# A rational MLP behind attention: the order of TensorE's products fixed by hand, in runs of one width

## The chip, the cores and the metric

One core of a Trainium2 chip runs the whole program. The metric is the device time of one execution in microseconds; the median of several runs counts. The engines are TensorE (matrix products, PE in the rows; its weight loads, PEld, overlap them), VectorE (DVE), ScalarE (ACT), GpSimd (POOL) and SyncE (SP), the last two issuing most of the DMAs.

## What is computed

Attention over 4 batches of 12 heads, 448 tokens and 64 columns a head, with a soft cap on the scores; its output, 1792 tokens by 768, goes through an MLP of 2048 hidden columns with a rational activation:

```python
x = attn_out.transpose(0, 2, 1, 3).reshape(B * S, H * D)   # 1792 x 768
h = x @ w_in                                               # 768 x 2048
P = a[0] + a[1] * h + a[2] * h * h + a[3] * h * h * h
Q = 1.0 + abs(b[0]) * abs(h) + abs(b[1]) * h * h
out = (P / (Q + 1e-6)) @ w_out                             # 2048 x 768
```

The change lies in the MLP. The two weight matrices come as 64-bit floats.

## The kernel before

All products keep nearly full precision by splitting each operand into a high and a low part and adding three products, high by high, high by low and low by high. The instructions of attention and MLP are first written down as operations with the keys that they read and write. `Plan.flush` (L118) then puts them in an order: it goes through a modelled time, and on each engine takes from the operations that are ready the one of smallest priority number, which is its place in the code less an `early`. Only the order comes from this; on the chip the engines wait for each other by semaphores.

**First stage.** The hidden columns are cut into 16 blocks of 128, two to a group g, and the tokens into two halves m of 896. A *unit* is one block of one half: `units` (L270) runs over g, then m, then the block y in the group, 32 units, four to a group. `stage1` (L764) computes a unit transposed, 128 hidden columns by 896 tokens: 6 pieces kc of the contraction, three products each, and each product for the token columns 0 to 512 and 512 to 896, because one product writes at most one of PSUM's banks. So a unit is 36 matmuls (L782), a 512-column and a 384-column one alternating, into two banks of one of the tiles `PS[0]`, `PS[1]`, `PS[2]` (`hbuf`, L787). Each kc is one operation of six matmuls, so that the plan can put other work between.

**Activation.** `rational` (L791) reads a unit from PSUM and makes G, high and low, in SBUF: six ScalarE and seven VectorE operations over 128x896 (L813 to L826), among them a logarithm (L818) and an exponential (L820) for the division.

**Second stage.** `stage2` (L828) computes one output *tile* of 128 tokens by 768 columns from the two units of a pair (the two blocks of one group and half): per block six matmuls of 384 columns (L851). There are seven tiles to a half. Tiles take turns in PSUM: `PS[1]`, or the pair of single banks `pv` and `mi`. A tile of the first half is copied to an `ev` buffer by ScalarE (L878), and a DMA on GpSimd's queue adds it to the output in memory; there are three such buffers. A tile of the second half is added to an accumulator in SBUF by VectorE (L884), or in the first group copied by ScalarE (L881).

**Weights.** `load_w` (L688) brings a weight tile as 64-bit words to one raw buffer by an SP DMA; `make_w` (L708) turns it into a 32-bit float (ScalarE L729, VectorE L731, L734, L737), and `split_w` (L752) writes its high half (ScalarE L759) and low half (VectorE L761) to a place in a ring of three for w_in or w_out.

**The order.** `mlp` (L902) writes units 0 and 1, then for each unit: its first stage, its rational, some waiting tiles of an earlier pair, and the conversion and next load that the table `todo` (L929) gives for this unit. What TensorE then does is up to the plan.

Of the kernel before, what the change touches and what calls it, by code (L numbers as in the profile page):

```python
# [58 lines left out]
TAIL_NS = 870  # L59
D_NS = 1430  # L60
E_S2 = 30

# [176 lines left out]
class Body:  # L239
# [468 lines left out]
    def make_w(self, f, which, park=None):  # L708
# [7 lines left out]
        X, xk = self.X, ("x", "M")  # L716
        n = self.DM
        if self.wide:


            XI = X.bitcast(I32)
            rk = self.rslot[(f, which)]
            if rk[1] == "A":
                X, xk = self.XA, ("x", "A")
                XI = X.bitcast(I32)
            wds = self.raw[rk[1:]].rearrange("p (n t) -> p n t", t=2)
            lo, hi = wds[:, :, 0], wds[:, :, 1]
            self.op(ACT, act_ns(n, False),
                    lambda: nc.scalar.activation(X, hi.bitcast(F32), AF.Abs, scale=2.0 ** -111), [rk], [xk])  # L729
            self.op(DVE, dve_ns(n, fast=True),  # L730
                    lambda: nc.vector.tensor_scalar(XI, XI, 3, 0x7FFFFFFF, ALU.logical_shift_left, ALU.bitwise_and),  # L731
                    [], [xk])
            self.op(DVE, dve_ns(n),
                    lambda: nc.vector.scalar_tensor_tensor(XI, hi, -0x80000000, XI, ALU.bitwise_and, ALU.bitwise_or),  # L734
                    [rk], [xk])
            self.op(DVE, dve_ns(n),
                    lambda: nc.vector.scalar_tensor_tensor(XI, lo, 29, XI, ALU.logical_shift_right, ALU.bitwise_or),  # L737
                    [rk], [xk])
            if park is not None:
                self.dma(SP, self.w32[park], X, [xk], [("w32", park)])  # L740
                return
# [10 lines left out]
    def split_w(self, f, which, X, xk):  # L752
        nc = self.nc
        hl, hk = self.wtile(f, which)
        n = self.DM

        c = self.ws if which == "w_in" else 1.0
        whole = self.rings.pop(hk, [])
        self.op(ACT, act_ns(n, False), lambda: nc.scalar.mul(hl()[:, 0], X, c), [xk], [(*hk, 0)] + whole)  # L759
        self.op(DVE, dve_ns(n),  # L760
                lambda: nc.vector.scalar_tensor_tensor(hl()[:, 1], X, c, f32(hl()[:, 0]), ALU.mult, ALU.subtract),  # L761
                [xk, (*hk, 0)], [(*hk, 1)])

    def stage1(self, u):  # L764

# [7 lines left out]
        po = self.PS[i].rearrange("p a b -> p (a b)")  # L773
        parts = slice(0, 512), slice(512, 2 * self.S)
        for kc in range(KC):
            h, lo = ([t[m][kc][:, ts] for ts in parts] for t in (self.XH, self.XL))
# [14 lines left out]
    def rational(self, u):  # L791
        nc = self.nc
        c = self.c
# [6 lines left out]
        h = self.PS[s].rearrange("p a b -> p (a b)")[:, 0:n].rearrange("p (a b) -> p a b", a=2)  # L800
        hk = [("ps", s)]

# [25 lines left out]
    def stage2(self, g, m, t):  # L828
# [6 lines left out]
        tt = slice(128 * t, 128 * t + 128)  # L835
        last = g == self.NG - 1

        end = s == 1 and (m, g, t) == (self.B // 2 - 1, self.NG - 1, len(self.acc) - 1)
        halves = []
        for y in range(self.NCH):  # L840
# [15 lines left out]
            if not end:  # L856
                self.op(PE, 6 * 174, lambda run=run: run((0, 1)), keys, pk)
            else:
                halves.append((run, keys))
        for n in range(2 if end else 0):  # L860
            for run, keys in halves:
                self.op(PE, 3 * 174, lambda run=run, n=n: run((n,)), keys, pk[n:n + 1])
        acc, ws = self.acc[t], self.ws
        ie = self.nev % len(self.ev)
        ev = self.ev[ie]
# [36 lines left out]
    def mlp(self, rest):  # L902
# [22 lines left out]
        for kc in range(self.KC - 2, self.KC):  # L925
            self.split_x(1, kc)
        pend = []
        last = len(self.units) - 1
        todo = [[(("w_in", 2), ("w_out", 1), ("w_out", 2), ("w_in", 3))[2 * m + y]] for _, m, y in self.units]  # L929
        todo = [[(which, g * self.NCH + d) for which, d in l] for l, (g, _, _) in zip(todo, self.units)]  # L930
        todo[0], todo[1] = [("w_out", 0)], todo[1] + todo[0]
        for u, (g, m, y) in enumerate(self.units):
            if u > 1 and u < last:
                self.stage1(u)
            self.rational(u)
            if u == last - 1:
                self.stage1(last)
            k = len(pend) // (self.NCH - y)
            for a in pend[:k]:
                self.stage2(*a)  # L940
            pend = pend[k:]

            for which, f in todo[u]:
                self.make_w(f, which)
            for which, f in todo[u + 1][:1] if u < last else ():
                self.load_w(f, which)
            if y == self.NCH - 1:
                pend = [(g, m, t) for t in range(NTT)]
        for a in pend:
            self.stage2(*a)  # L950

    def memory(self):
# [83 lines left out]
        if self.wide:  # L1036
            t, o = take(2 * self.DM)
            keys("M", o, (("raw", "M", 0), 2 * self.DM))
            keys("P", o, (("parked", 0), self.DM), (("parked", 1), self.DM))
            self.raw["M", 0] = t.bitcast(I32)  # L1040

        t, o = take(896)
# [11 lines left out]
        self.X, o = take(self.DM)  # L1054
        keys("M", o, (("x", "M"), self.DM))


# [172 lines left out]
```

## Time and profile before

| | us |
|---|---|
| median of 3 runs | 674.99 |
| lowest, highest | 674.13, 675.17 |
| the profiled execution | 673.43 |
| its span, first to last instruction | 671.6 |
| TensorE busy | 658.4 (98%) |
| VectorE busy | 546.7 (81%) |
| ScalarE busy | 445.7 (66%) |

Attention runs to about 192 us, the MLP from there to the end. In each row of a timeline the first number is the start in us from the span's start and the second the length from there to the end of the last of the merged instructions; a bracket gives the engine's idle time ahead and what ended it. Matmuls overlap, so the busy time of TensorE says only that it has work; how fast it goes is read from the distance between starts. The line numbers in the rows are those of the code above.

### The profile page before, as it was taken

To read this page: it belongs to the slowest core of one execution; us is meant where nothing else is said; L and a number is where in the kernel's file an instruction comes from. 1 tells how busy PE (TensorE), PEld (TensorE's weight loads), DVE (VectorE), ACT (ScalarE), POOL (GpSimd) and SP (SyncE) were. 2 spreads that over 40 slices of the span, in tenths; PEclk is the share of its full clock that TensorE was granted. 3 is DMA by queue.
4 is the path that set the end of the run, shared out by engine and by line. 5 is a ranking of instruction groups with operands and counts; after the bars stand their busy time and mean duration, and the time that the engine had idled before them with its cause. 6 is when DMAs were issued, how large, how long until landed. Compare 5 with 4: busy or idle time off the path is not lost.

```text
span 671.6 us, 9841 instructions
## 1 busy us (share of the span) xinstructions
PE 658.4 (98%) x3852; PEld 542.5 (81%) x3852; DVE 546.7 (81%) x677; ACT 445.7 (66%) x531; POOL 97.0 (14%) x159
## 2 busy tenths in 40 slices
PE   7999999999999999999999999999999999999996
PEld 4555455555468899999999999999999999999996
DVE  4789899998869987887877997887799789779753
ACT  5799989998948867674476556447655644764560
POOL 4023323233200000120011012001101200110030
PEclk9999999999999999999999999999999999999999
DMA  7757767763131351482167129216712831670086
GB/s 175 173 127 163 171 158 157 145 138 95 30 104 29 124 182 48 88 151 68 56 154 144 48 57 184 66 51 159 143 47 58 157 92 51 160 143 0 1 128 207
DMA packets 79896, 74.44 MB, mean 111 GB/s; under 512 B 49377, under 2 KB 68065, under 8 KB 79841
## 3 DMA queue, kind: packets, MB, share of 16 engines
q1 hardware_dynamic: 68240, 48.68, 25.8%
q0 software_dynamic: 10448, 24.80, 21.8%
q8 instruction: 32, 0.52, 0.3%
q10 hardware_dynamic: 1152, 0.25, 0.2%
q14 instruction: 24, 0.19, 0.1%
HBM read 47.98 MB, written 25.65 MB: 110 GB/s over the span
## 4 chain that ended last, share of the span: by engine, by line
issue 57%; PE 24%; POOL 6%; ACT 5%; DMA 3%; DVE 3%; SPq 0%; ACTq 0%; POOLq 0%; DVEq 0%
PE ps L413 8%; POOL out_dram L286 6%; PE mi L497 4%; PE pv L497 3%; ACT etiles L443 2%; PE mi L542 2%; ACT ps L425 2%; PE ps L334 1%; PE pv L514 1%; DMA out_dram<-arena_f 1%; PE ps L851 1%; PE ps L357 1%; PE ps L782 1%; ACT arena_r L586 1%; DMA arena_f<-in_k_dram 1%
## 5 line engine op out<-in xcount | busy, mean ns | idle before, releaser
L782 PE MATMUL ps<-arena_r,ring 128*128 128x512 f32 (+1 forms) x1152 | 246.3, 368 | 0.0
L782 PEld LDWEIGHTS ps<-arena_r,ring 128*128 128x128 f32 x1152 | 209.4, 188 | 26.2 <-issue 0.7
L286 POOL DMA_DIRECT2D out_dram<-arena_f x49 | 43.1, 893 | 425.8 <-ACT arena_f L878 421.7
L851 PE MATMUL ps<-arena_r,etiles 128*128 128x384 f32 x462 | 90.0, 335 | 0.9 <-ACT arena_f L878 0.5
L825 ACT CAST etiles<-arena_f 128x896 fp32r<-128x896 f32 x32 | 30.1, 942 | 91.0 <-DVE arena_f L824 91.0
L425 ACT ACTIVATE ps<-ps 128x896 f32<-128x896 f32 x84 | 74.3, 907 | 19.4 <-PE ps L413 18.9
L851 PEld LDWEIGHTS ps<-arena_r,etiles 128*128 128x128 f32 x462 | 81.0, 188 | 2.6 <-ACT arena_f L878 0.9
L443 ACT ACTIVATE etiles<-ps,acap 128x896 f32<-128x896 f32 x84 | 82.4, 1011 | 1.1
L851 PE MATMUL pv<-arena_r,etiles 128*128 128x384 f32 x231 | 77.0, 335 | 0.0
L851 PE MATMUL mi<-arena_r,etiles 128*128 128x384 f32 x231 | 76.9, 334 | 0.0
L413 PE MATMUL ps<-arena_r 64*128 64x448 f32 x576 | 71.0, 380 | 4.5 <-DVE arena_r L342 2.0
L413 PEld LDWEIGHTS ps<-arena_r 64*128 64x128 f32 x576 | 50.6, 184 | 29.6 <-ACT etiles L443 6.8
L813 ACT ACTIVATE arena_f<-ps,b 128x896 f32<-128x896 f32 x32 | 32.3, 1009 | 40.7 <-PE ps L782 40.3
L817 DVE SCALAR_TENSOR_TENSOR arena_f<-arena_f,bab 128x896 f32<-128x896 f32 x32 | 36.7, 1147 | 24.4 <-ACT arena_f L814 24.3
L826 DVE TENSOR_TENSOR etiles<-arena_f,etiles 128x896 fp32r<-128x896 f32 x32 | 34.8, 1088 | 18.4 <-ACT etiles L825 17.6
L822 DVE SCALAR_TENSOR_TENSOR arena_f<-arena_f,one 128x896 f32<-128x896 f32 x32 | 36.7, 1148 | 16.0 <-ACT arena_f L820 15.9
L851 PEld LDWEIGHTS pv<-arena_r,etiles 128*128 128x128 f32 x231 | 43.3, 188 | 0.7
L851 PEld LDWEIGHTS mi<-arena_r,etiles 128*128 128x128 f32 x231 | 43.3, 188 | 0.0
L851 PE MATMUL ps<-ring,etiles 128*128 128x384 f32 x210 | 42.3, 336 | 0.2
L818 ACT ACTIVATE arena_f<-arena_f,qb 128x896 f32<-128x896 f32 x32 | 33.7, 1054 | 8.0 <-DVE arena_f L817 7.9
L851 PEld LDWEIGHTS ps<-ring,etiles 128*128 128x128 f32 x210 | 36.9, 188 | 1.3 <-ACT arena_f L878 0.8
L815 ACT ACTIVATE arena_f<-ps,a 128x896 f32<-128x896 f32 x32 | 35.4, 1106 | 3.5 <-DVE arena_f L823 3.5
(123 smaller groups left out, 1027.1 us busy)
## 6 DMA issues: line engine op xcount, KB each, us to landing
out_dram<-arena_f POOLq DMA_DIRECT2D x49, 384.0 KB, 6.0
arena_f<-in_moe_w_out_dram SPq DMA_DIRECT2D x16, 768.0 KB, 4.1
arena_f<-in_moe_w_in_dram SPq DMA_DIRECT2D x16, 768.0 KB, 6.0
out_dram<-arena_f SPq DMA_DIRECT2D x13, 384.0 KB, 3.2
ring<-in_q_dram SPq DMA_DIRECT2D x44, 112.0 KB, 4.3
arena_r<-dn POOLq DMA_DIRECT2D x20, 224.0 KB, 4.7
ring<-in_k_dram SPq DMA_DIRECT2D x33, 128.0 KB, 4.5
ring<-in_v_dram SPq DMA_DIRECT2D x11, 384.0 KB, 3.8
```

Source lines behind the costliest of these rows:

```text
L286: self.op(eng, (625 if local else 450) if eng == SP else 1050, lambda: e.dma_start(out, in_, **accum), r, w, nbytes=nbytes, **kw)
L413: m = nc.tensor.matmul(self.PS[i][:, j, 0:448], st[r], mv[r], start=y == 0, stop=y == len(ops) - 1)
L425: self.op(ACT, act_ns(896, True), lambda: nc.scalar.activation(ps, ps, AF.Tanh), ["table"], pk)
L443: self.op(ACT, act_ns(size, sk[0][0] == "ps", 1), lambda: nc.scalar.activation(e, src, AF.Exp, scale=acap), sk + ["table"], [ek])
L497: m = nc.tensor.matmul(po[64 * j:64 * j + 64, 0:448], raw["v"][:, 2 * x + j, 64 * c:64 * c + 64], tiles[c][0][:, j], start=c == 0, stop=False)
L782: r = nc.tensor.matmul(po[:, ts], w[:, y, kc], x, start=kc == 0 and z == 0, stop=kc == KC - 1 and z == 2)
L815: self.op(ACT, act_ns(n, True, 2), lambda: T.activation(A, h, AF.Identity, scale=a[:, 3:4], bias=a[:, 2:3]), hk, ak)
L817: self.op(DVE, dve_ns(n, 1), lambda: stt(Bt, C, bab[:, 1:2], Bt, ALU.mult, ALU.add), ck + ["bab"], bk)
L818: self.op(ACT, act_ns(n, False, 1), lambda: T.activation(C, Bt, AF.Ln, scale=TWO_M64, bias=qb), bk + tb, ck)
L822: self.op(DVE, dve_ns(n, 1), lambda: stt(Bt, Bt, one, C, ALU.add, ALU.mult), ck, bk)
L826: self.op(DVE, dve_ns(n), lambda: V.tensor_tensor(GL(), A, f32(GH()), ALU.subtract), ak + K("gh", ig), K("gl", ig))
L851: r = nc.tensor.matmul(po[n][:, 0:384], st, mv[:, 384 * n:384 * n + 384], start=(y == 0 and x == 0), stop=(y == self.NCH - 1 and x == 2))
```

## The change

Units from 4 on issue all 18 products of 512 columns first and then the 18 of 384, each as one operation. Behind each run a fixed number of second-stage tiles follows (`PER`: two and two, but none and three behind every fourth unit, one left over before it). These operations and the tiles share a key `turn`, so the plan may not change their order on TensorE. A pair's tiles are queued when the second unit behind it begins. Of a group's w_out tiles, one is converted in the group's first unit and one in its third, ahead of that unit's rational, which is about a unit later than before; conversions get an `early` of 10. The last group's tiles of the first half have six `ev` buffers in place of three, in memory of the raw buffer and of `X`.

```diff
+E_W = 10
+PER = ((2, 2), (2, 2), (2, 2), (0, 3))
+LAST = (0, 0)
+FIRST = 3
...
+        early = E_W * (park is None and f >= len(EARLY))
...
-    def stage1(self, u):
+    def stage1(self, u, between=None):
...
+        if between:
+            for x, ts in enumerate(parts):
+                def run(ts=ts):
+                    w = wi().rearrange("p s (k f) -> p s k f", f=128)
+                    for kc in range(KC):
+                        h, lo = (t[m][kc][:, ts] for t in (self.XH, self.XL))
+                        for z, (y, mv) in enumerate(((0, h), (0, lo), (1, h))):
+                            r = nc.tensor.matmul(po[:, ts], w[:, y, kc], mv,
+                                                 start=kc == 0 and z == 0, stop=kc == KC - 1 and z == 2)
+                    return r
+                self.op(PE, 18 * (174, 229)[x == 0], run,
+                        [(*wk, 0), (*wk, 1)] + [(n, m, kc) for n in ("xh", "xl") for kc in range(KC)],
+                        [(("ps", "psb")[x], i), "turn"])
+                between(x)
+            return
...
-        hk = [("ps", s)]
+        hk = [("ps", s), ("psb", s)]
...
+        turn = [] if not g and not m else ["turn"]
...
-        ie = self.nev % len(self.ev)
+        ie = (t + 3) % 6 if last else self.nev % 3
...
-        todo = [[(("w_in", 2), ("w_out", 1), ("w_out", 2), ("w_in", 3))[2 * m + y]] for _, m, y in self.units]
-        todo = [[(which, g * self.NCH + d) for which, d in l] for l, (g, _, _) in zip(todo, self.units)]
-        todo[0], todo[1] = [("w_out", 0)], todo[1] + todo[0]
+        todo = [(("w_out", 0), ("w_in", 2), ("w_out", 1), ("w_in", 3))[2 * m + y] for _, m, y in self.units]
+        todo = [(which, g * self.NCH + d) for (which, d), (g, _, _) in zip(todo, self.units)]
+        tiles = []
+
+        def pop(n):
+            for a in tiles[:n]:
+                self.stage2(*a)
+            del tiles[:n]
+
         for u, (g, m, y) in enumerate(self.units):
-            if u > 1 and u < last:
-                self.stage1(u)
+            if u % 2 and u > 2:
+                g0, m0, _ = self.units[u - 3]
+                tiles += [(g0, m0, t) for t in range(NTT)]
+            if u > 1:
+                self.stage1(u, u > 3 and (lambda x: pop(PER[u % 4][x] if u < last else LAST[x])))
+            if u > 3 and u % 4 == 2:
+                self.make_w(todo[u][1], todo[u][0])
             self.rational(u)
...
+            if u == 3:
+                pop(FIRST)
+            self.make_w(todo[u][1], todo[u][0])
```

**TensorE, around a unit in the repeating part.** `ps_127`, `ps_128` and `ps_129` are the three PSUM tiles. Before, with the pairs that repeat left out between the two parts, the rows are:

```order
L851 MATMUL ps_128<-arena_r,etiles 128x384 x6
L851 MATMUL ps_128<-ring_2063,etiles 128x384 x6
L782 MATMUL ps_129<-arena_r,ring_1764 128x512
L782 MATMUL ps_129<-arena_r,ring_1764 128x384
...
L851 MATMUL pv<-arena_r,etiles 128x384
L851 MATMUL mi<-arena_r,etiles 128x384
```

Now, with the rest of a tile's `pv` and `mi` products left out, they are:

```order
L873 MATMUL ps_128<-ring_2063,etiles 128x384 x6
L873 MATMUL ps_128<-arena_r,etiles 128x384 x6
L788 MATMUL ps_129<-arena_r,ring_1764 128x512 x18
L873 MATMUL pv<-ring_2063,etiles 128x384
L873 MATMUL mi<-ring_2063,etiles 128x384
...
L788 MATMUL ps_129<-arena_r,ring_1764 128x384 x18
```

The eighteen pairs have become two runs, and between the runs of one unit stand two tiles.

**ScalarE, where three tiles of a first half follow a unit.** `b` and `a` mark the reads of a unit's result, `qb` and `eb` the logarithm and the exponential. Before, in a group of the repeating part:

```order
L813 ACTIVATE arena_f<-ps_129,b 128x896
L759 ACTIVATE ring_2063<-arena_f 128x768
L814 ACTIVATE arena_f<-ps_129 128x896
L815 ACTIVATE arena_f<-ps_129,a 128x896
L818 ACTIVATE arena_f<-arena_f,qb 128x896
L729 ACTIVATE arena_f<-arena_f 128x768
L878 ACTIVATE arena_f<-ps_128 128x768
L878 ACTIVATE arena_f<-pv 128x384
```

Now:

```order
L734 ACTIVATE arena_f<-arena_f 128x768
L834 ACTIVATE arena_f<-ps_127,b 128x896
L835 ACTIVATE arena_f<-ps_127 128x896
L836 ACTIVATE arena_f<-ps_127,a 128x896
L900 ACTIVATE arena_f<-ps_128 128x768
L846 CAST etiles<-arena_f 128x896
L900 ACTIVATE arena_f<-pv 128x384
```

The eviction of the first tile (`ps_128`) stood behind the reads, the logarithm and a conversion's first step; now it stands behind three reads of the unit that ended just ahead of it, and ahead of the cast of the unit before.

**VectorE, at the second w_out tile of a group.** The last row of a conversion is the low half (L761, now L767). Before:

```order
L824 SCALAR_TENSOR_TENSOR arena_f<-arena_f 128x896
L737 SCALAR_TENSOR_TENSOR arena_f<-arena_f 128x768
L826 TENSOR_TENSOR etiles<-arena_f,etiles 128x896
L761 SCALAR_TENSOR_TENSOR arena_r<-arena_f,arena_r 128x768
L817 SCALAR_TENSOR_TENSOR arena_f<-arena_f,bab 128x896
```

Now:

```order
L742 SCALAR_TENSOR_TENSOR arena_f<-arena_f 128x768
L838 SCALAR_TENSOR_TENSOR arena_f<-arena_f,bab 128x896
L906 SCALAR_TENSOR_TENSOR arena_f<-pv,arena_f 128x384
L906 SCALAR_TENSOR_TENSOR arena_f<-mi,arena_f 128x384
L767 SCALAR_TENSOR_TENSOR arena_r<-arena_f,arena_r 128x768
L840 TENSOR_TENSOR arena_f<-ps_129,arena_f 128x896
```

The low half stood ahead of the next unit's first operation (L817) and now stands behind it (L838) and behind the two evictions of a tile.

## Rows read from the trace of the kernel before

**Rows 1.** Busy us (and instructions) of each engine in a stretch; clock, DMA share, GB/s.
```profile
core 0: us, PE busy (x) PEld busy (x) DVE busy (x) ACT busy (x) POOL busy (x), PEclk, DMA share, GB/s
...
396.00:454.00 58.00, 58.00 (x310) 54.59 (x309) 48.20 (x55) 33.62 (x42) 6.21 (x7) 1.00 0.46 97
```

**Rows 2.** TensorE's waits from 200 us on: in total, times, longest.
```profile
PE ps L851 <- ACT arena_f L878: 0.5, 1, 0.5
PE ps L851 <- DVE arena_f L821: 0.4, 1, 0.4
```

**Rows 3.** Timeline of TensorE: one unit, and the tile behind it.
```profile
252.24 7.59 PE L782 MATMUL ps<-arena_r,ring 128*128 128x512 f32 x36
259.67 2.25 PE L851 MATMUL ps<-arena_r,etiles 128*128 128x384 f32 x12
261.76 0.33 PE L851 MATMUL pv<-arena_r,etiles 128*128 128x384 f32 x1
```

**Rows 4.** TensorE's groups by form, 280 to 628 us, and the unit's first product alone.
```profile
L782 PE MATMUL ps<-arena_r,ring 128*128 128x512 f32 x431 | 171.2, 397 | 0.0
L782 PE MATMUL ps<-arena_r,ring 128*128 128x384 f32 x430 | 145.3, 338 | 0.0
L851 PE MATMUL ps<-arena_r,etiles 128*128 128x384 f32 x330 | 64.3, 334 | 0.0
...
L782 PE MATMUL ps<-arena_r,ring 128*128 128x512 f32 x1 | 0.4, 390 | 0.0
```

**Rows 5.** Timeline of TensorE in the warm-up.
```profile
7.72 0.63 PE L389 MATMUL ps<-arena_r 128*128 128x512 f32 x2
...
7.95 0.40 PE L389 MATMUL ps<-arena_r 128*128 128x512 f32 x1
```

**Rows 6.** Timelines of TensorE and ScalarE where three tiles follow a unit.
```profile
275.43 1.21 PE L851 MATMUL ps<-ring,etiles 128*128 128x384 f32 x6
...
279.60 1.20 PE L851 MATMUL ps<-ring,etiles 128*128 128x384 f32 x6
...
275.63 1.01 ACT L813 ACTIVATE arena_f<-ps,b 128x896 f32<-128x896 f32 x1 [1.31 <-PE ps L782]
...
278.32 0.82 ACT L878 ACTIVATE arena_f<-ps 128x768 f32<-128x768 f32 x1
```

**Rows 7.** Timelines of ScalarE and VectorE: a rational's two ends, a split's two halves.
```profile
305.07 1.01 ACT L813 ACTIVATE arena_f<-ps,b 128x896 f32<-128x896 f32 x1 [3.18 <-PE ps L782]
...
335.42 0.83 ACT L759 ACTIVATE ring<-arena_f 128x768 fp32r<-128x768 f32 x1
...
318.55 1.08 DVE L826 TENSOR_TENSOR etiles<-arena_f,etiles 128x896 fp32r<-128x896 f32 x1
...
336.29 0.96 DVE L761 SCALAR_TENSOR_TENSOR ring<-arena_f,ring 128x768 fp32r<-128x768 f32 x1 [1.00 <-ACT ring L759]
```

**Rows 8.** DMA issues of the page: count, KB each, us to landing.
```profile
out_dram<-arena_f POOLq DMA_DIRECT2D x49, 384.0 KB, 6.0
arena_f<-in_moe_w_out_dram SPq DMA_DIRECT2D x16, 768.0 KB, 4.1
```

**Rows 9.** Timelines of TensorE and VectorE at the first tiles.
```profile
219.12 1.34 PE L851 MATMUL ps<-arena_r,etiles 128*128 128x384 f32 x6 [0.37 <-DVE arena_f L821]
...
225.25 1.21 PE L851 MATMUL ps<-arena_r,etiles 128*128 128x384 f32 x6
...
228.05 2.35 PE L851 MATMUL ps<-arena_r,etiles 128*128 128x384 f32 x12 [0.55 <-ACT arena_f L878]
...
224.07 1.09 DVE L826 TENSOR_TENSOR etiles<-arena_f,etiles 128x896 fp32r<-128x896 f32 x1
```

**Rows 10.** ScalarE's waits from 196 us on, and weight loads in the last group.
```profile
ACT arena_f L878 <- DMA out_dram<-arena_f: 4.9, 4, 2.1
...
648.90 1.00 PEld L851 LDWEIGHTS ps<-ring,etiles 128*128 128x128 f32 x6 [0.41 <-ACT arena_f L878]
...
653.46 0.99 PEld L851 LDWEIGHTS ps<-ring,etiles 128*128 128x128 f32 x6 [0.40 <-ACT arena_f L878]
```

More of the change, by code (lines that the diff above doesn't have):

```diff
@@ L856, in stage2 @@
             if not end:
-                self.op(PE, 6 * 174, lambda run=run: run((0, 1)), keys, pk)
+                self.op(PE, 6 * 174, lambda run=run: run((0, 1)), keys, pk + turn)
             else:
@@ L861, in stage2 @@
             for run, keys in halves:
-                self.op(PE, 3 * 174, lambda run=run, n=n: run((n,)), keys, pk[n:n + 1])
+                self.op(PE, 3 * 174, lambda run=run, n=n: run((n,)), keys, pk[n:n + 1] + turn)
         acc, ws = self.acc[t], self.ws
-        ie = self.nev % len(self.ev)
+        ie = (t + 3) % 6 if last else self.nev % 3
         ev = self.ev[ie]
@@ L926, in mlp @@
             self.split_x(1, kc)
-        pend = []
         last = len(self.units) - 1
-        todo = [[(("w_in", 2), ("w_out", 1), ("w_out", 2), ("w_in", 3))[2 * m + y]] for _, m, y in self.units]
-        todo = [[(which, g * self.NCH + d) for which, d in l] for l, (g, _, _) in zip(todo, self.units)]
-        todo[0], todo[1] = [("w_out", 0)], todo[1] + todo[0]
-        for u, (g, m, y) in enumerate(self.units):
-            if u > 1 and u < last:
-                self.stage1(u)
-            self.rational(u)
[L936 to L950, printed above, removed]
+        todo = [(("w_out", 0), ("w_in", 2), ("w_out", 1), ("w_in", 3))[2 * m + y] for _, m, y in self.units]
[5 more added lines that the diff above has]
+            del tiles[:n]
+        for u, (g, m, y) in enumerate(self.units):
+            if u % 2 and u > 2:
[5 more added lines that the diff above has]
+                self.make_w(todo[u][1], todo[u][0])
+            self.rational(u)
+            if u == 3:
+                pop(FIRST)
+            self.make_w(todo[u][1], todo[u][0])
+            if u < last and todo[u + 1][::-1] not in self.made:
+                self.load_w(todo[u + 1][1], todo[u + 1][0])
+        g0, m0, _ = self.units[last]
+        pop(len(tiles))
+        for t in range(NTT):
+            self.stage2(g0, m0, t)
     def memory(self):
@@ L1040, in memory @@
             self.raw["M", 0] = t.bitcast(I32)
+            spare = [(t[:, self.DM * x:self.DM * (x + 1)], o + 4 * self.DM * x) for x in range(2)]
+        else:
+            spare = [take(self.DM) for _ in range(2)]
         t, o = take(896)
@@ L1055, in memory @@
         keys("M", o, (("x", "M"), self.DM))
+        for n, (t, o) in enumerate([*spare, (self.X, o)]):
+            keys("E", o, ([("ev", 3 + n, 0), ("ev", 3 + n, 384)], self.DM))
+            self.ev.append(t)
         base[0] = 0
```

13 lines of the change are left out of this document (7 added, 6 removed).

## The prediction

> **What bounds the kernel now.** I read four views, from the whole to the single instruction. First the busy times over 58 us in the middle of the MLP stage [rows 1]: TensorE is busy for all of it, VectorE for 48.2 us, ScalarE for 33.6 us, at a granted clock of 1.00. Then the waits of TensorE from 200 us to the end [rows 2]: two, 0.9 us together, neither in the middle. So in the repeating part nothing is waited for; the time there is the number of matmuls times the distance from one start to the next, and only a change of that distance, or a new wait, can move it. Third, TensorE's timeline around one unit of the first stage [rows 3]: its 36 matmuls start between 252.24 and 259.67, 7.43 us, 206.4 ns each, so 413 ns for a pair of one 512-column and one 384-column product. The second-stage tile behind it, 12 products of 384 columns, takes 2.09 us (259.67 to 261.76), 174 ns each.
>
> The fourth view is the length of single records [rows 4]. A matmul overlaps the next, so its record is longer than the distance; in the second stage it is 334 ns against 173 to 174, a surplus of 161. Inside a first-stage unit, where the widths alternate, the 512-column record is 397 and the 384-column one 338. But the first 512-column product of a unit, which comes behind a row of 384-column ones, is 390. So the same instructions are 7 and 4 ns longer where widths alternate: 11 ns a pair.
>
> **The change, part by part.**
>
> *Runs of one width.* Units 4 to 31, 28 of 32, issue eighteen 512-column products and then eighteen of 384 columns. A 384-column product among its like takes 173.5 ns. For 512 columns among their like there are two rows: the record of 390 less the surplus of 161 gives 229, and in the warm-up two such products start at 7.72 and 7.95, 0.23 us apart [rows 5]. I take 229. A unit is then 18 x (229 + 173.5) = 7.25 us, with 0.01 for the one change of width left in it 7.26, against 7.44 (7.43, and the last pair's 8 ns that fall on the next tile). That is 0.185 us a unit and 28 x 0.185 = **5.2 us**, all of it on the path, since TensorE never waits there. The bounds: if 512 columns keep the 237 that they have in the alternation (413 less 176), 18 x 28 x 8 ns = 4.0 us of this is lost; if the 0.23 is a rounded 0.225, it is 2 us more. I keep 229 because two independent rows give it.
>
> *The order of units and tiles.* Nothing is added or taken away on any engine: the same matmuls, evictions and conversions in another order. A fixed order costs if something is late, so I walk through one group of four units with durations from the rows. A tile takes 2.08 us, a 512-run 4.12, a 384-run 3.12.
> - Evictions. With two tiles, a run, two tiles, a bank is written again one run and one tile after its tile ended: at least 3.12 + 2.08 = 5.2 us. Before, tiles often followed each other directly and a bank had 2.08 us. These waits become easier.
> - The one place with three tiles in a row is behind unit 4g+3. The third needs the bank of the first 2 x 2.08 = 4.16 us after the unit ended, and ScalarE stands there with three reads of the unit's own result first. The kernel before has this place too [rows 6]: the unit ends at 275.43, the first read starts at 275.63, the eviction at 278.32, and it lasts 0.82, to 279.14; the third tile starts at 279.60 without a gap. Margin 0.46 us, and in the new order the same three reads stand ahead of the eviction in most groups. I count zero.
> - G, the input of a tile. From the end of unit 4g+1 to the first tile that reads its G, TensorE has 2 tiles, a 512-run, 2 tiles, a 384-run, 1 tile and a whole unit to do, 25 us. The chain from a unit's first read to its G took 305.07 to 318.55 + 1.08 with evictions between [rows 7], 14.6 us. Zero.
> - w_out a unit later. The second w_out tile of a pair is now converted in unit 4g+2 and overwrites a ring place that the last tile of the previous group still reads. Let the unit end at T. ScalarE does three reads (0.2 + 2.7 us, as in rows 6) and then the high half, 0.83: T + 3.8. VectorE has a first operation and two evictions ahead and then writes the low half, 0.96 [rows 7]: T + 5.0. The first product that reads it comes one tile, one unit and half a tile after T: 2.08 + 7.26 + 1.04 = T + 10.4. Margin 5.4 us. Behind the waiting ScalarE instruction stand this unit's logarithm and exponential, due some 15 us later. The loads on SP's queue alternate w_out and w_in singly now, where they came in twos; that of this tile (4.1 us to land [rows 8]) is issued some 15 us ahead of T. Zero.
>
> *The start.* Before, TensorE stops twice [rows 9]: idle 0.37 us at 219.12, and 0.55 at 228.05. To each come the surplus of 0.16, which the record of the matmul ahead hides, and about 0.12 for the slower row behind it (1.34 against 1.21 us for six): 0.65 and 0.83, together 1.48. Unit 3 ended at 225.25 with 2.08 us of tile halves and the first stop inside; now it runs through, to about 222.5, and the first halves of two tiles follow, to 224.6. The second halves need the G that VectorE finishes at 224.07 + 1.09 = 225.16 (the order up to there is the same): a wait of 0.6 us. They end at 227.3. The third tile needs the first eviction, ahead of which ScalarE has a logarithm and a read of unit 3, 1.0 us each; from 224.8 on it ends at 227.5, a wait of 0.2. With slower rows behind both, 1.0 against 1.48: **0.45 us** gained. Bounds: all 1.48 gained, or 0.5 lost if one more ScalarE operation stands in the way.
>
> *The last group.* Before, three buffers take the last seven tiles of the first half, and ScalarE waits four times, 4.9 us, for transfers to empty them; through it TensorE's weight loads stop for 0.41 at 648.90 and 0.40 at 653.46 [rows 10], some 0.35 us of TensorE each once the overlap is off. With six buffers the reuse for six of the tiles is gone, and the seventh reuses one after 12 us, over a landing of 6.0 [rows 8]. **0.7 us.** What is late next are the transfers themselves, which have to be over only when the last output lands, and that waits for the last tile.
>
> **The sum.** 5.2 + 0.45 + 0.7 = 6.35 us. The profiled execution took 673.43 us with a span of 671.6: 667.1 for it. The median of the runs stands 1.56 us above it, at 674.99: **668.6**.
>
> The Trainium skill, "TensorE: Matmul & The Clock Gate", section "Back-to-back issue gap", gives the distance at full clock as columns / 2.4 GHz plus 2.5 ns, whatever the neighbours are. By it a pair takes 378 ns in either order and the runs bring nothing: 673.8 in the sum above. The pair takes 413 here, so the trace disagrees with the size; whether it disagrees on the order is the first rival.
>
> **The rivals.**
> - *The distance belongs to the product, not to its neighbours.* The 390 would be a matter of the boundary between the stages alone. For it: only one place shows 512 behind 512, and to 10 ns. Against: the 384-column record changes with its neighbours too, 338 against 334. Then only start and tail are left, 674.99 - 1.15 = 673.8, a change that can't be told from none. 10%.
> - *The third tile waits.* If ScalarE has a conversion or the previous unit's last cast ahead of the eviction at the place with three tiles, its 0.9 to 1.0 us exceed the margin of 0.46 by 0.5, in seven groups 3.5 us: 668.6 + 3.5 = 672.1, still faster. In the first and the last group the order has that cast there. 14%.
> - *Slower: the late w_out.* The second w_out tile misses its product. For that its chain has to slip by more than 5.4 us; TensorE then loses the excess in each of seven groups, and at 6.3 us of slip it has lost the whole gain. VectorE would have to be behind by six or seven operations at T, in a stretch where I count some 14 us of its work in 15.6 us of TensorE's. At 7.1 us, 7 x 1.7 = 12: 668.6 + 12 = 680.6. Against it: VectorE idles 9.8 of 58 us [rows 1], and by the same walk it catches up within each group. 6%.
> - *The change does not do what it says.* Excluded on TensorE: the built order has the runs.
>
> **How the numbers follow.** Forecast 70% (its own range 666.8 to 670), third tile 14%, no gain from runs 10%, slower 6%. The range leaves out the last two and the far edge of the second, and below it takes in part of the lower bound of the 512-column distance and a start without a stop: 666.8 to 672.0. About 0.2%, 1.35 us, is what a measurement of this kernel can tell from no change. Faster 70 + 14 = 84% and 1 from the near edge of the first rival, 0.85; same 0.09; slower 0.06.
>
> **What would show it.** In the profile of the changed kernel the 512-column record should read 390 and the 384-column one 334; a 512-run should take 4.12 us and a 384-run 3.12. TensorE should have next to no wait between 230 us and the end, and ScalarE none for transfers in the last seven tiles. A record of 397 inside a run makes the main term wrong. A repeated idle of TensorE behind unit 4g+3 with ScalarE's eviction as releaser is the third tile; one in the middle of a first tile, with the low half of w_out as releaser, is the slower rival.

## The result, and the profile after

The changed kernel takes 668.71 us (median of 5 runs, 666.99 to 670.11) beside 674.14 for the kernel before on the same chip (673.29 to 675.17). The medians differ by 5.43 us. The ratio of the runs on record is 0.9904, with a 95% interval from 0.9891 to 0.9918, which is 5.5 to 7.3 us. The forecast was 668.6. The profiled execution took 666.99 us with a span of 665.0, at a granted clock of 0.998; before it was 673.43 and 671.6.

TensorE's groups by form, 280 to 628 us, in the changed kernel (out<-in, shape, count, then busy us and mean ns of one record, then idle time before them). They answer to [rows 4].

```profile
L788 PE MATMUL ps<-arena_r,ring 128*128 128x512 f32 x432 | 102.8, 391 | 0.0
L788 PE MATMUL ps<-arena_r,ring 128*128 128x384 f32 x428 | 78.4, 334 | 0.0
L873 PE MATMUL ps<-arena_r,etiles 128*128 128x384 f32 x336 | 65.0, 334 | 0.0
```

The records of the first stage went from 397 and 338 ns to 391 and 334. What counts is the distance from one start to the next. The timeline of TensorE shows it over a whole unit (the first row), over three tiles of which the third starts at 284.94, and over a 512-run and a 384-run with two tiles behind each:

```profile
273.51 7.43 PE L788 MATMUL ps<-arena_r,ring 128*128 128x512 f32 x36
280.78 1.20 PE L873 MATMUL ps<-ring,etiles 128*128 128x384 f32 x6
...
284.94 1.20 PE L873 MATMUL ps<-ring,etiles 128*128 128x384 f32 x6
...
287.02 4.28 PE L788 MATMUL ps<-arena_r,ring 128*128 128x512 f32 x18
291.14 0.33 PE L873 MATMUL pv<-ring,etiles 128*128 128x384 f32 x1
...
295.33 3.28 PE L788 MATMUL ps<-arena_r,ring 128*128 128x384 f32 x18
...
298.45 0.33 PE L873 MATMUL pv<-ring,etiles 128*128 128x384 f32 x1
```

The unit takes 7.27 us (273.51 to 280.78) where that of [rows 3] took 7.43. The 512-run takes 4.12 us (287.02 to 291.14), two tiles follow, and the 384-run takes 3.12 (295.33 to 298.45). All three are within 0.01 us of the forecast, and no wait stands between. In the whole MLP TensorE's list of waits has no row for the repeating part and none for the last group. The chain of work that ended last runs over TensorE for 86% of the span:

```profile
PE 86%; ACT 6%; DVE 3%; DMA 2%; issue 1%; SPq 0%; ACTq 0%; DVEq 0%
```

### The profile page after: what moved, and what is told of

The parts are those of the page before. It is cut to its first block, busy times and chain, and to the rows that moved or that the text cites. A ratio compares the mean times of both kernels' runs of the same rounds, so it can differ in the third digit from the quotient of the medians.

```text
span 665.0 us, 9868 instructions
## 1 busy us (share of the span) xinstructions
PE 652.5 (98%) x3852; PEld 541.4 (81%) x3852; DVE 547.0 (82%) x677; ACT 442.9 (67%) x531; POOL 96.3 (14%) x159
## 4 chain that ended last, share of the span: by engine, by line
PE 86%; ACT 6%; DVE 3%; DMA 2%; issue 1%; SPq 0%; ACTq 0%; DVEq 0%
PE ps L788 31%; PE ps L873 17%; PE mi L873 9%; PE pv L873 9%; PE ps L417 8%; PE mi L501 4%; PE pv L501 3%; ACT etiles L447 2%; PE mi L546 2%; ACT ps L429 2%; PE ps L338 1%; PE pv L518 1%; PE ps L361 1%; ACT arena_r L590 1%; DMA arena_f<-in_k_dram 1%
## 5 line engine op out<-in xcount | busy, mean ns | idle before, releaser
L788 PE MATMUL ps<-arena_r,ring 128*128 128x512 f32 (+1 forms) x1008 | 210.8, 363 | 0.0
L788 PEld LDWEIGHTS ps<-arena_r,ring 128*128 128x128 f32 x1008 | 182.2, 188 | 19.2
L734 ACT ACTIVATE arena_f<-arena_f 128x768 f32<-128x768 f32 x32 | 29.3, 915 | 45.9 <-DMA arena_f<-in_moe_w_out_dram 31.4
L838 DVE SCALAR_TENSOR_TENSOR arena_f<-arena_f,bab 128x896 f32<-128x896 f32 x32 | 36.8, 1150 | 20.6 <-ACT arena_f L835 20.5
```

The lines of the kernel that those rows point to most:

```text
L788: r = nc.tensor.matmul(po[:, ts], w[:, y, kc], mv, start=kc == 0 and z == 0, stop=kc == KC - 1 and z == 2)
L838: self.op(DVE, dve_ns(n, 1), lambda: stt(Bt, C, bab[:, 1:2], Bt, ALU.mult, ALU.add), ck + ["bab"], bk)
```

## Experiments: what makes an alternating pair dear

Two kernels take the parts of the change singly, two change the widths, one takes away the buffers, and two serve to read distances only (they ran once each, 693.93 and 667.28 us, and are not in the table). The changed kernel was run a second time. The ratios are to the kernel before on the same chip: 674.14 us for the changed kernel, 675.01 for "changed, again" and for three buffers, 674.60 for the other four. The last column is the stretch from the start of the first matmul of the MLP to the start of the last one, read from the trace. It leaves out attention and the last transfers, which vary from run to run.

| kernel | median us | ratio to before, 95% interval | first to last matmul, us |
|---|---|---|---|
| before | 674.14 | | 473.24 |
| changed | 668.71 | 0.9904 (0.9891 to 0.9918) | 466.46 |
| changed, again | 668.91 | 0.9911 (0.9895 to 0.9927) | 466.65 |
| its order, widths alternating | 673.72 | 0.9988 (0.9977 to 1.0000) | 471.40 |
| before, with runs | 670.77 | 0.9945 (0.9929 to 0.9960) | 469.25 |
| changed, 448 + 448 alternating | 673.90 | 0.9990 (0.9975 to 1.0005) | 471.48 |
| changed, 448 + 448 in runs | 673.38 | 0.9982 (0.9971 to 0.9994) | 471.53 |
| changed, three buffers | 669.89 | 0.9926 (0.9913 to 0.9939) | 467.02 |

My theory going in: a matmul takes longer when the one ahead of it has another width. The rivals: the order and the buffers bring the gain; or the change of bank does.

**The order without the runs.**

```diff
-            for x, ts in enumerate(parts):
+            for x in range(2):
...
-                    for kc in range(KC):
+                    for kc in range(3 * x, 3 * x + 3):
...
+                            for ts, o in zip(parts, mv):
...
```

> The changed kernel with its order, its tiles between the products, its conversions and its six buffers kept; only the widths inside units 4 to 31 alternate again: the first part of a unit is nine pairs of a 512-column and a 384-column product (kc 0 to 2), the second part nine more (kc 3 to 5), with the same number of tiles behind each part. Theory 1 (a change of width costs about 10 ns a pair): units take 7.43 us again in place of 7.25, the 512-column record reads 397 and the 384-column one 338, and 28 units x 0.175 us = 4.9 us are lost against the changed kernel: 673.6 us, ratio to the kernel before 0.999. Rival (the fixed order and the buffers bring the gain, and the runs don't matter): as the changed kernel, 668.7 us, ratio 0.992.

Measured: 673.72 us, and 4.94 us over the changed kernel in the stretch (471.40 against 466.46). The groups by form and one whole unit:

```profile
L789 PE MATMUL ps<-arena_r,ring 128*128 128x512 f32 x420 | 167.0, 398 | 0.0
L789 PE MATMUL ps<-arena_r,ring 128*128 128x384 f32 x420 | 142.2, 338 | 0.0
```

```profile
274.51 7.59 PE L789 MATMUL ps<-arena_r,ring 128*128 128x512 f32 x36
281.94 1.21 PE L874 MATMUL ps<-ring,etiles 128*128 128x384 f32 x6
```

The records are those of before, and so is the unit, 7.43 us. Of the 4.94 us, 0.10 lie at the start: by the starts of the matmuls the stop there costs 0.42 us in this kernel and 0.32 in the changed one. That leaves 4.84 us for the runs, 4.84 / 28 = 0.173 us a unit. All else in the change is worth 473.24 - 471.40 = 1.84 us, nearly all of it stops that are gone at the start and in the last group.

**The runs without the order.**

```diff
+        if u > 3:
+            for x, ts in enumerate(parts):
+                def run(ts=ts):
...
+                self.op(PE, 18 * (174, 229)[x == 0], run,
...
+                        [(("ps", "psb")[x], i)])
+            return
...
```

> The kernel before with one edit: units 4 to 31 issue eighteen 512-column products as one operation and then eighteen 384-column ones as another. The planner stays free to put what it likes between them; w_out conversions stand where they stood, and the last group has three buffers. Theory 1: the records read 390 and 334, a unit takes 7.26 us in place of 7.43, about 28 x 0.175 = 4.9 us gained, 669.2 us, ratio to the kernel before 0.993, unless the coarser operations make a new wait; TensorE's stops at the start (1.5 us) and in the tail (0.7 us) are still there. Rival (the order brings it): 674, ratio 1.000.

Measured: 670.77 us, 3.99 us under before in the stretch. The records are 391 and 334, as in the changed kernel. But TensorE has two new waits in the middle, here in its timeline (in the bracket the idle time, and what ended it):

```profile
323.33 1.32 PE L865 MATMUL ps<-ring,etiles 128*128 128x384 f32 x6 [0.27 <-DVE arena_f L898]
...
556.83 1.31 PE L865 MATMUL ps<-arena_r,etiles 128*128 128x384 f32 x6 [0.46 <-DVE arena_f L898]
```

Left to itself the planner puts tiles in a row, and a tile waits until VectorE has read its bank (L898). From the starts, the rows concerned are late by 0.54 and 0.74 us. The account closes: 4.8 from the runs, minus 1.3 for the two waits, plus 0.4 because the start loses that much less, is 3.9, beside 4.0 measured. So the runs bring most of the gain in either order. The changed kernel has neither of the two waits and so doesn't pay the 1.3 us back. It moves both the tiles and the conversions that stand ahead of VectorE's reads; which of the two removes the waits was not tested.

**Equal widths.** A unit's 896 columns also divide into 448 and 448, and then no width changes inside a unit. In one kernel the two halves alternate, in the other each is a run. The edit that both share:

```diff
-        parts = slice(0, 512), slice(512, 2 * self.S)
+        po = {0: self.PS[i][:, 0, 0:self.S], 1: self.PS[i][:, 1, 0:self.S]}
+        parts = slice(0, self.S), slice(self.S, 2 * self.S)
...
-        h = self.PS[s].rearrange("p a b -> p (a b)")[:, 0:n].rearrange("p (a b) -> p a b", a=2)
+        h = self.PS[s][:, :, 0:self.S]
...
```

> The order of the changed kernel, but every unit of the first stage is 36 products of 448 columns each (a unit's 896 tokens cut in halves) in place of 512 and 384, and the two halves alternate: one goes to one bank, the next to the other, with the same weights twice in a row. It tells apart what makes an alternating pair dear. Theory 1, the change of width: with equal widths there is none, so the distance is that of a run, about (229 + 173.5)/2 = 201 ns, a unit takes 7.25 us, also in units 0 to 3; time as the changed kernel's or up to 1 us less: 668 us, ratio to the kernel before 0.991. Theory 2, the change of bank or the weights used twice in a row: 206 ns, a unit 7.43 us, about 673.6 us, ratio 0.999.

> The changed kernel with 448 + 448 columns in place of 512 + 384: a run of eighteen into one bank, a run of eighteen into the other from unit 4 on, and alternating in units 0 to 3. Theory 1 (a change of width is what costs): distance about 201 ns everywhere, units 0 to 3 gain 0.18 us each and the 28 units lose the one change of width that they have left, together about 1 us under the changed kernel: 667.7 us, ratio to the kernel before 0.990. Theory 2 (change of bank): no gain in units 0 to 3, 668.7 us.

Measured: 673.90 and 673.38 us. Both are as slow as the alternation of 512 and 384. TensorE's group of the first stage in the one and in the other, 280 to 628 us, and a whole unit of the second:

```profile
L789 PE MATMUL ps<-arena_r,ring 128*128 128x448 f32 x844 | 181.0, 368 | 0.0
```

```profile
L788 PE MATMUL ps<-arena_r,ring 128*128 128x448 f32 x846 | 181.4, 368 | 0.0
```

```profile
276.03 7.60 PE L788 MATMUL ps<-arena_r,ring 128*128 128x448 f32 x36
283.46 1.21 PE L873 MATMUL ps<-ring,etiles 128*128 128x384 f32 x6
```

From unit 4 on it is 7.43 us a unit, 206.65 ns from start to start once settled, whether the banks alternate or not. The change of bank is out, since both kernels agree and one of them has next to none. So is the use of the same weights by both halves in a row, which the first kernel has and the second not. My theory falls too: in the second kernel eighteen equal products follow each other and still take 6.6 ns more than the 200 that lie midway between the settled distances of 384 and 512 columns (173.3 and 226.7, below).

But 206.65 is not the distance of 448 columns everywhere. In units 0 to 3, which alternate in both kernels and have no tiles between them, the same products come faster. TensorE's timeline of the first of the two kernels:

```profile
193.81 29.45 PE L804 MATMUL ps<-arena_r,ring 128*128 128x448 f32 x144
223.10 1.22 PE L874 MATMUL ps<-arena_r,etiles 128*128 128x384 f32 x6
```

That is 29.29 us for four units, of which the second and the third take 7.30 and 7.29, where 512 and 384 in turn take 7.44. One by one the distances are 199, 207, 202, 203 ns, over and over for 140 products, 202.7 on average. From unit 4 on the same kernel has the same two halves in turn behind a row of 384-column products, and there they take 206 to 207. So a row of equal products of one width, in one order, can hold either of two patterns.

**Many patterns in one kernel.** Since TensorE never waits in these groups, one program can show a pattern per group. In this edit and the next `a` and `b` are the 512 and the 384 columns, `one` is the eighteen products of a run, and `cut` makes slices of columns.

```diff
...
+            runs = lambda *w: [[(*j, t) for t in c for j in one] for c in w]
+            mix = lambda n: [(*j, t) for k in range(0, 18, n) for t in parts for j in one[k:k + n]]
+            seq = {1: runs([a], [b]), 2: [mix(2)[:20], mix(2)[20:]], 3: [mix(6)[:24], mix(6)[24:]],
+                   4: runs(cut(0, 480), cut(448, 896)), 5: runs(cut(0, 416, 448), cut(448, 832, 896)),
+                   6: runs([a], cut(512, 768, 896)), 7: runs(cut(0, 256, 512), cut(512, 704, 896))}[g]
...
```

> A measuring kernel: the order of the changed kernel, but in each of the groups 1 to 7 the first stage cuts and orders its products in another way; only the distances from one matmul's start to the next are of interest, the whole time is not. Group 1: runs of 512 and 384 (229 and 173.5 expected). Group 2: two of 512, two of 384 in turn, so half as many changes of width as in single alternation. Group 3: six and six. Group 4: a run of 480 columns, 32 of them computed twice, and one of 448. Group 5: runs of 416, 32, 384 and 64. Group 6: 512, 256, 128. Group 7: 256, 256, 192, 192. Theory 1 (each change of width has a price): single alternation costs 413 a pair against 400 to 403 in runs, so with every second product changing the pair costs 407, with every sixth 402. Theory 2 (a product is charged for the odd part of its width, and 448, which took 206.65 in runs of its like, shows it: columns / 2.4 + 13.3 = 200 would be expected from 512 and 384): groups 2 and 3 still cost 413 a pair, or at least don't fall in proportion to the changes; 480 and 416 columns show a surcharge like that of 448, some 6.6 ns over 213.3 and 186.7. Under either the products under 384 columns may be held at some floor by the weight loads, whose records are 187 ns long: 173 for all of them if a load can't be overlapped by another, less if it can.

Measured, first on the changes of width. The timeline of TensorE at a whole unit of group 1 (runs), of group 2 (two and two) and of group 3 (six and six), each with the tile behind it:

```profile
276.87 7.43 PE L796 MATMUL ps<-arena_r,ring 128*128 128x512 f32 x36
284.13 1.20 PE L882 MATMUL ps<-ring,etiles 128*128 128x384 f32 x6
```

```profile
335.57 7.59 PE L796 MATMUL ps<-arena_r,ring 128*128 128x512 f32 x36
343.00 1.21 PE L882 MATMUL ps<-arena_r,etiles 128*128 128x384 f32 x6
```

```profile
394.03 7.46 PE L796 MATMUL ps<-arena_r,ring 128*128 128x512 f32 x36
401.33 2.24 PE L882 MATMUL ps<-arena_r,etiles 128*128 128x384 f32 x12
```

7.26, 7.43 and 7.30 us. Two and two has half as many changes of width as single alternation and costs the same 7.43. So it is no price per change. Six and six has nearly four fifths of the gain (0.132 of 0.166 us a unit by the starts).

Next the rows of other widths, of groups 4 and 5 by form (417 to 477 and 477 to 549 us):

```profile
L796 PE MATMUL ps<-arena_r,ring 128*128 128x448 f32 x67 | 14.5, 368 | 0.0
L796 PE MATMUL ps<-arena_r,ring 128*128 128x480 f32 x54 | 12.2, 378 | 0.0
```

```profile
L796 PE MATMUL ps<-arena_r,ring 128*128 128x416 f32 x54 | 10.6, 350 | 0.0
L796 PE MATMUL ps<-arena_r,ring 128*128 128x64 f32 x72 | 8.4, 272 | 0.0
L796 PE MATMUL ps<-arena_r,ring 128*128 128x32 f32 x54 | 6.2, 258 | 0.0
```

The mean of a row hides how its distances go one by one. Here they are, from the starts of the records, for units from 4 on. They repeat to the nanosecond or two in each unit:

| columns, row of equal products | distances ns | settled mean | above columns / 2.4 GHz |
|---|---|---|---|
| 512, behind 384 | 229 233 236 224 231 236 228 233 230, then 227 227 226 | 226.7 | 13.3 |
| 480 | 215 213, then 221 212 221 212 | 216.6 | 16.6 |
| 448 | 201, then 207 206 207 | 206.65 | 20.0 |
| 416 | 187 184, then 191 189 190 183 | 188.3 | 15.0 |
| 384 | 173 173 174 | 173.3 | 13.3 |
| 256 | 117 to 121 seven times, then 120 | 120.0 | 13.3 |
| 64 | 112 111 112 | 111.7 | 85.0 |
| 512 and 384 in turn, per pair | 237.6 and 175.8 | 413.3 | 40.0 |

A row of equal products runs into a pattern after at most nine products: one distance, or two or four that come round. With 512, 384 and 256 columns the pattern costs 13.3 ns over the columns, with 448 it costs 20 here, and so does the alternating pair on average (24.3 and 15.8). From 192 columns down the distance no longer falls: rows of 192, 128, 64 and 32 columns all come to 111 to 112 ns on average. That is so inside a row only. The first product of 32 or 64 columns behind a long one takes 27 to 30 ns, and the first of 384 columns behind such a row 258 to 266. Theory 2's surcharge is there for 416 and 480 columns, but far smaller than the 6.6 that it put: 1.7 and 3.3.

**How a run is entered.**

```diff
...
+            split = lambda n, *w: [(*j, slice(w[k], w[k + 1])) for j in one[:n] for k in range(len(w) - 1)] + run1(a, n)
+            seq = {1: [split(1, 0, 256, 512), run1(b)], 2: [split(1, 0, 128, 512), run1(b)], 3: [run1(b), run1(a)],
+                   4: [[(0, 0, b)] + run1(a), run1(b, 1)], 5: [split(2, 0, 256, 512), run1(b)],
+                   6: [split(1, 0, 448, 512), run1(b)], 7: [split(1, 0, 320, 512), run1(b)]}[g]
...
```

> A second measuring kernel: runs as in the changed kernel, but the way into the 512-run differs from group to group, to see whether the ten slow distances at the head of a run (229, 233, 236, 224, 231, 236, 228, 233, 230, then 226.7 from the tenth on; 43 ns a run above 18 x 226.7) belong to the entry. Group 1: the first 512-column product cut into 256 + 256. Group 2: into 128 + 384. Group 3: the 384-run first, the 512-run behind the two tiles. Group 4: one 384-column product of the unit first, then the 512-run. Group 5: the first two products cut into 256 + 256. Group 6: the first into 448 + 64. Group 7: into 320 + 192. Theory (the distance depends on a state that the products ahead have left, and a row of equal products settles into its own pattern): groups 3 and 4 enter from 384 columns as now and show the same ten distances; at least one of the cuts leaves another state, and the run behind it settles at once or in another way. Rival (the ten slow distances are a matter of the place in the run, such as its first operands): the same head in every group. A cut costs 240 for two of 256 against 229, so there is nothing to win beyond some 30 ns a unit, 0.8 us in all.

Measured, distances from the starts again:

| way in | then the 512-column products | 512-run with its entry, us |
|---|---|---|
| from 384 columns (groups 3 and 4) | 229 233 236 224 231 236 228 232 231 227 | 4.121 |
| 256 + 256 | 235 233 236 224 231 236 228 232 231 227 | 4.135 |
| 128 + 384 | 228 232 231 227 | 4.155 |
| two cut into 256 + 256 | 236 233 227 | 4.115 |
| 448 + 64 | 310 230 233 236 224 231 236 228 232 231 227 | 4.207 |
| 320 + 192 | 257 236 228 233 231 226 | 4.134 |

The rival is out: the slow head is no matter of the place in the run. In five of the six ways the sequence is the same, and a run joins it at its start or further on: behind 128 + 384 at its "228 232 231", behind 320 + 192, after a first 257, at its "236 228 233 231". Behind two products cut in halves it is another, 236 233, and settles at the third. The distance depends on a state that the products ahead have left. There is nothing to win with it: the best way in saves 6 ns a unit.

**Three buffers in place of six.**

```diff
-        ie = (t + 3) % 6 if last else self.nev % 3
+        ie = self.nev % 3
```

> The changed kernel with three buffers for the tiles of the last group's first half, as before, in place of six. By the prediction the six are worth 0.7 us: ScalarE waits for the transfers out of the buffers again, four times, some 5 us, TensorE's weight loads stop twice for 0.4 us, and the time is 0.7 us over the changed kernel's on the same chip, 669.5 if that reads 668.8. Rival: in the new order the last tiles follow each other otherwise, the wait falls where TensorE has work left, and the time is the same.

> The changed kernel itself once more, as the measure for the run with three buffers on the same chip, and for its start: whether the stop of 0.65 us that the prediction set for G of the second unit comes back when attention's last transfer lands later (VectorE's first operation behind it stood at 200.0 us before and at 199.2 in the first profile of the changed kernel). Expected 668.7 us, ratio to the kernel before 0.991.

Measured: 669.89 us against 668.91 for the changed kernel on the same chip. The two intervals overlap, so the times alone don't decide. The trace does: ScalarE waits for transfers again (total, times, longest), and TensorE's weight loads stop twice in the last group, though shorter than in [rows 10].

```profile
ACT arena_f L900 <- DMA out_dram<-arena_f: 4.4, 4, 1.7
```

```profile
647.16 0.19 PEld L873 LDWEIGHTS pv<-ring,etiles 128*128 128x128 f32 x1 [0.28 <-ACT arena_f L900]
647.54 0.19 PEld L873 LDWEIGHTS mi<-ring,etiles 128*128 128x128 f32 x1 [0.19 <-ACT arena_f L900]
```

The stretch is 467.02 against 466.65 us, and the starts of the matmuls put the two stops, which follow each other in one tile, at 0.43 us together: in the new order the six buffers are worth about 0.4 us, at one place and not two, where 0.7 was expected.

## Why the prediction was right, step by step

The sum was -6.35 us; the profiled execution fell by 6.44 and its span by 6.6. In the stretch the fall is 473.24 - 466.46 = 6.78. Outside it, attention took 0.3 us less and the end behind the last matmul 0.4 more.

| term | predicted us | measured us | from |
|---|---|---|---|
| runs of one width | 5.2 | 4.8 | alternating kernel less changed one, the start left out |
| start | 0.45 | 1.13 and 0.94 | stops of before, 1.45 by the starts, less those in two profiles of the changed kernel |
| last group | 0.7 | 0.7 (0.4 by the buffers) | two stops of before, gone; three-buffer kernel |
| order, evictions, G, w_out | 0 | 0 | no wait in the list |

**That the sum came so near** is in part luck. The runs brought 0.4 us less than was put, the start 0.5 to 0.7 more, and attention and the end, which the sum put at nothing, together cost 0.2: these nearly cancel. The 668.6 was also reckoned from a median before of 674.99; the kernel before took 674.14 beside the result, from where the same sum gives 667.8, 0.9 under the measured median.

**The main term** was right in size to 8% and too wide in its reason. The 512-column distance was taken as 229, with two rows for it [rows 4, 5]; the mean in the runs is 228.9 (4.12 / 18). That the two agree is chance: the two rows show 229 near the head of a row, while a run begins with nine of 224 to 236 and settles at 226.7. 384 columns were taken as 173.5 and take 173.3 once settled; behind a 512-run the first seven take 27 ns more together (171 175 178 185 176 181 174), where 0.01 us was allowed; that is most of the hundredth of a microsecond a unit that was missing. The first rival, that the distance belongs to the product and not to its neighbours, is out: the same product takes 229 in a run and 237.6 in the alternation. But the sentence "longer where widths alternate", read as a law, would have promised a gain to 448 + 448 in every unit, and from unit 4 on that has none. What carried the forecast was not the law but two places in the trace of before that had the beginning of the new order: a 512-column product behind a row of 384-column ones, and two behind each other in the warm-up.

By the rule of the Trainium skill that the prediction weighed ("TensorE: Matmul & The Clock Gate", section "Back-to-back issue gap", columns / 2.4 GHz plus 2.5 ns, there given as the gap of an isolated matmul) the runs would have brought nothing. The trace disagrees on the order as well as on the size: a pair takes 413 ns in alternation and 403 in runs, against 378 by the rule.

**The start** is where a step failed. The prediction let the second halves of the first two tiles wait 0.6 us for G of unit 1, since VectorE ends it at 225.16 and TensorE is there at 224.6. There is no such stop in either profile. In the first VectorE ends G at 224.35, 0.02 us behind the start of the half tile; in the second, at 225.01 against 224.79, the stop should have been there. The low half that VectorE makes is read only by the fifth and sixth product of a half tile; the first four read the high half, which ScalarE's cast has ready earlier, at 222.93 + 0.95 = 223.88 in the second profile. The fifth product starts 4 x 0.174 = 0.7 us after the first, by the prediction's own numbers at 225.3, behind the 225.16. The kernel with 448 columns in runs shows it, where VectorE is later: the half tile starts at 225.56 on TensorE, and it is its fifth weight load that waits, at 226.42. The timeline of its weight loads, and VectorE's operation:

```profile
226.42 0.30 PEld L873 LDWEIGHTS ps<-arena_r,etiles 128*128 128x128 f32 x2 [0.32 <-DVE etiles L847]
...
225.27 1.09 DVE L847 TENSOR_TENSOR etiles<-arena_f,etiles 128x896 fp32r<-128x896 f32 x1
```

The other stop, of the third tile behind the first eviction, came about as put: 0.2 with 0.12 for the slower row behind it was forecast, and the starts show 0.32 and 0.51 us. In the second profile it stands in TensorE's timeline as

```profile
227.27 2.38 PE L873 MATMUL ps<-arena_r,etiles 128*128 128x384 f32 x12 [0.24 <-ACT arena_f L900]
```

**The third tile** did not wait. In the group shown above ScalarE does two reads, the last unit's cast and then the eviction:

```profile
280.98 1.01 ACT L834 ACTIVATE arena_f<-ps,b 128x896 f32<-128x896 f32 x1 [1.75 <-PE ps L788]
281.89 0.91 ACT L835 ACTIVATE arena_f<-ps 128x896 f32<-128x896 f32 x1
282.68 0.94 ACT L846 CAST etiles<-arena_f 128x896 fp32r<-128x896 f32 x1
283.52 0.82 ACT L900 ACTIVATE arena_f<-ps 128x768 f32<-128x768 f32 x1
```

The eviction ends at 284.34 and the third tile starts at 284.94: 0.60 us, where 0.46 was read from before. The case that the rival feared, the cast ahead of the eviction, is just this group. The cast had pushed one of the three reads behind the eviction, so the count stayed at three.

**The late w_out** kept its margin. The unit ahead ended at 273.51 - 2.08 = 271.43; the low half of the second w_out tile was written by VectorE from 275.97:

```profile
275.97 0.96 DVE L767 SCALAR_TENSOR_TENSOR arena_r<-arena_f,arena_r 128x768 fp32r<-128x768 f32 x1 [0.17 <-ACT arena_r L765]
```

That is done 5.5 us after the unit's end (5.0 was forecast), and the first product that reads it stands in the half tile from 281.82, 10.4 us after it. What is new is a wait of ScalarE for a w_out transfer at the head of a conversion, in total, times, longest. The time that these loads take to land, from 200 us on, stands below it:

```profile
ACT arena_f L734 <- DMA arena_f<-in_moe_w_out_dram: 31.4, 6, 6.9
```

```profile
DMA to landing us min/median/max: 4.2/5.3/9.1
```

Before, no such load took over 4.2 us, and the prediction went by 4.1 [rows 8]. The wait costs nothing, as no wait of TensorE follows from it. That ScalarE stands up to 6.9 us behind a transfer was not foreseen, though; the prediction looked only at the operations queued behind the unit's reads.

**The last group** lost both its stops, which the starts of before put at 0.37 and 0.35 us. The run with three buffers parts them: about 0.4 us is the buffers, and the other 0.3 came with the order. The prediction put all 0.7 to the buffers; its size is right, its reason only for the larger part.

**What stays open.** The runs show that the distance depends on a state, that rows of equal products settle, and into what. They don't show what the state is, nor why 448 columns hold one pattern in units 0 to 3 and another behind. No kernel tried the runs in units 0 to 3 as well; by 0.173 us a unit they would bring at most 0.7 us, half of what a measurement of this kernel can tell. Nor did one keep 448 + 448 in units 0 to 3 alone, where it takes 0.14 us a unit less than 512 and 384 in turn. None of the variants in the table beat the changed kernel.

## What to carry to other kernels

Where an engine never waits, the time is the distance from start to start, and a new order is best priced by a place in the old trace that already has it, and has it for long enough to settle; a law made from two such places ("a change of width costs") should be tried on a second pattern before it is used. When an operation of several instructions waits for several inputs, look which of its instructions reads the late one. A run that is cheaper on TensorE pays in full only if no new wait comes with it, here 1.3 us of 4.8.

## What the hardware showed that was not expected

- The distance between matmuls with a weight load each is not a function of width alone: 448 columns in a row take 206.65 ns from unit 4 on and 202.7 in units 0 to 3 of the same kernel, and 512 columns settle at 226.7 in a row and take 237.6 in turn with 384. From unit 4 on, widths of 512 + 384 beat 448 + 448 by 0.17 us a unit, in runs only.
- A row of 512-column products behind 384-column ones needs nine products to settle, and repeats the same nine distances each time, to a nanosecond or two.
- In a row, short products don't come closer than about 112 ns: 192, 128, 64 and 32 columns all take that. The Trainium skill, "TensorE: Matmul & The Clock Gate", section "LDWEIGHTS (loading the stationary operand)", puts a weight load at its columns / 1.2 ns, 107 ns for 128 columns. The trace agrees within 5 ns, if the floor is the load; that it is the load no run here shows, and the loads' own records in the row of 32 columns are 192 ns long and start 112 ns apart.
